# A written-out schedule is replaced by another: two input transfers change places, weights are requested sooner, and the last output halves get a bank each

## The chip, the cores and the metric

The kernel runs on one core of a Trainium2 chip. The metric is the device time of one execution in microseconds (us). Five engines work side by side, each through its own instructions in a fixed order: PE multiplies matrices into PSUM (eight banks), DVE and ACT do elementwise work and empty PSUM, POOL does elementwise work in SBUF and issues some transfers, SP issues the other transfers.

## What is computed

The reference is a gated linear attention over four batches and eight heads of width 48, and a feed-forward layer with SiLU behind it:

```python
f = 1.0 / (1.0 + np.exp(-f_logit))
state = np.zeros((B, H, D, D))
for t in range(S):
    state = f[:, :, t, :, None] * state + np.einsum('bhd,bhe->bhde', k[:, :, t], v[:, :, t])
    y[:, :, t] = np.einsum('bhd,bhde->bhe', q[:, :, t], state)
x = y.transpose(0, 2, 1, 3).reshape(3072, 384)
h = x @ w_in                       # 384 x 2048
out = (h * sigmoid(h)) @ w_out     # 2048 x 384
```

B is 4, H is 8, S is 768, D is 48. The output is 3072 x 384 in float32.

## The kernel before

The sequence is cut into chunks of 128 tokens. A *unit* is one chunk of one batch with all heads, and there are 24; two units make a *pair*, and there are twelve. Pairs 0 to 3 are the first two chunks of one batch each (form T, interleaved tokens), pairs 4 to 11 are the same chunk of two batches (form N).

All work is written out in one table, `PLAN`. A word such as `qg.0.1:G` names the work (`qg`), the pair (0), the unit in the pair (1), the engine (G is POOL, V is DVE, A is ACT, P is PE, S is SP) and, if it makes a new value, the buffer that it takes. The kernel emits the words one after another, so the table fixes the order on each engine. The framework adds the waits between engines. Nothing is reordered later: an instruction that waits holds back all behind it on its engine. The four input transfers that stand first in the table are emitted ahead of the constants.

The words, in the order of the data flow through a pair:

- `f`, `k`, `q`, `v` load the inputs (L241, on SP). `wi` and `wo` load a quarter of `w_in` and of `w_out`, cast to bf16 on the way (L216 and L219, on POOL).
- `E` and `L` (L248, L260, L263) make the logarithm of the gate, `cs` (L324, L331) its running sum on PE, `a` and `ia` (L336) the exponentials of the sum with either sign, `al` (L278, L338) those of the chunk's whole sum.
- `qg` and `ki` (both L341) are the products q by `a` and k by `ia`, on DVE or POOL. `vb` casts v to bf16.
- `tq` (L348) transposes both products on PE, and `qkc` (L185 on ACT, L187 on DVE) copies them out of PSUM; for most later units `qkD` (L360) does both with one transposing transfer.
- `sc` (L369, L373) are the scores, `at` (L377) the masked scores on DVE, `d` (L297, L406) the chunk's addition to the state, `sd` and `su` (L410, L420) the new state, `yi` and `y` (L285, L385, L389) the outputs of the attention, `yc` their cast.
- `yT` and `xc` (L397, L185, L187), or one transposing transfer `yD` (L401), bring them into the layout of the feed-forward layer.
- `mi` (L271) is an eighth of the first layer's product for a pair, into one bank; in pairs 0 and 1 it goes unit by unit. `si` (L276) is its SiLU on ACT. ACT has to load another function table (L513) when it turns from exponentials to SiLU or back.
- `mo` (L306) is a quarter of the second layer's sum for a unit, so four words fill one output bank. `oc` copies it out and `so` (L316, L318) stores it. The last pair's `mo`, `oc` and `so` work on halves of the columns: the fourth number of `mo.11.0.3.1` and the third of `oc.11.0.1` are the half.
- `idle.512.11` runs eleven matmuls without a use (L465).

Buffers rotate: eight PSUM banks `pb`, five exponentials `x`, five products `qk`, and so on. Both halves of the last units' outputs share one bank:

```python
nc.tensor.matmul(at("o", P, i)[:, cols], at("hT", P)[:, n, i * C:(i + 1) * C], w_out_sb[:, n, cols], start=(n == 0), stop=(n == NT - 1))
```

Of the kernel before, what the change touches and what calls it, by code (L numbers as in the profile page):

```python
# [41 lines left out]
tq.1.0:P:2 q.3.0:S:3 a.2.0:A:3 qg.1.1:G: sc.0.0:P:3,4 qkc.1.0:A:1 sc.0.1:P:6,7 at.0.0.1:V:0 k.3.0:S:3 wi.1:G: at.0.0.0:V: E.3.0:A:1 idle.512.2::5
tq.1.1:P:5 at.0.1.0:V:1 wi.2:G: d.1:P:1,4 qkc.1.1:A: v.2.0:S:2 su.1.0:V:0 wi.0:G: at.0.1.1:V: al.2:A:2 L.3.0:A:0 idle.512.3::2 sc.1.0:P:2,3 ki.2.0:G:4
sc.1.1:P:6,1 at.1.0.1:V:2 vb.0.0:A:2 cs.3.1:P:5 vb.0.1:A:3 at.1.1.0:V:3 qg.2.0:G: al.3:A:3 ia.2.1:A:2 d.0:P:7,3 at.1.1.1:V: a.2.1:A:0 cs.3.0:P:6
ia.3.1:A:4 su.0.0:V:0 qg.2.1:G:2 y.0:P:0,1 a.3.0:A:1 at.1.0.0:V: yc.0.0:A:0 yi.0.1:P: tq.2.0:P:7 a.3.1:A:3 wi.3:G: yc.0.1:V:1 ia.3.0:A:0 y.1:P:0,2
wo.0:G: ki.2.1:V: yc.1.0:A:2 yT.0.0:P:5 sd.0.1:V:0 yi.1.1:P: yT.0.1:P:1 yc.1.1:A:0 tq.2.1:P:6 xc.0.0:V:0 wo.1:G: xc.0.1:A: qkc.2.0:V:0 v.3.0:S:3
yT.1.0:P:0 yT.1.1:P:3 xc.1.0:A:1 mi.0.2.0:P:2 qkc.2.1:V: su.0.1:G:0 xc.1.1:A: mi.0.3.0:P:5 mi.1.3.0:P:1 sd.1.1:V:1 mi.1.3.1:P: qg.3.0:V:3 wo.2:G:
mi.0.2.1:P: sc.2.1:P:7,0 si.1.3:A:0 wo.3:G: qg.3.1:V:0 sc.2.0:P:3,6 at.2.1.1:V:0 mi.1.5.1:P:4 mi.1.2.1:P:1 at.2.0.0:V:1 mi.1.2.0:P: at.2.0.1:V:
mi.0.3.1:P: mi.1.4.1:P:0 at.2.1.0:V: mi.1.4.0:P: mi.0.5.0:P:3 si.1.4:A: mi.1.0.0:P:6 mi.1.1.1:P:7 mi.1.0.1:P: f.5.0:S:0 mi.1.5.0:P: si.1.0:A:
mi.0.1.1:P:0 si.0.3:A:1 mi.0.1.0:P: mi.0.5.1:P: si.1.5:A: ki.3.0:G: mi.0.0.0:P:6 si.0.1:A: mi.0.6.0:P:5 mi.0.0.1:P: su.1.1:G:0 mi.0.7.1:P:4 si.0.0:A:  # L50
mi.0.7.0:P: si.0.2:A: mi.0.6.1:P: ki.3.1:G: mi.1.1.0:P: si.0.6:A: mi.1.7.0:P:0 tq.3.0:P:6 mi.1.7.1:P: qkc.3.0:A:1 mi.0.4.0:P:2 tq.3.1:P:5 si.1.7:A:
mi.0.4.1:P: f.4.0:S:1 mo.0.0.0:P:6 qkc.3.1:A: mo.0.1.0:P:0 si.1.1:A: mi.1.6.1:P:5 si.0.5:A: mi.1.6.0:P: si.1.2:A: mo.1.1.0:P:7 si.1.6:A: mo.0.1.1:P:
si.0.4:A: si.0.7:A: sc.3.1:P:3,1 sc.3.0:P:5,2 at.3.1.0:V:2 vb.2.0:A:4 mo.0.1.2:P: at.3.1.1:V: mo.1.1.1:P: at.3.0.0:V:3 mo.0.0.1:P: q.4.0:S:4
mo.0.1.3:P: vb.3.0:V:5 mo.1.1.2:P: vb.3.1:V:6 oc.0.1:V:0 mo.1.1.3:P: at.3.0.1:V: v.5.0:S:4 mo.0.0.2:P: vb.2.1:V:2 v.5.1:S: oc.1.1:V:1 d.2:P:4,3
so.1.1:G: y.2:P:1,5 su.2.0:V:0 v.4.0:S:5 d.3:P:0,2 E.4.0:A:0 sd.2.1:V:0 y.3:P:7,4 yc.3.0:V:1 yi.2.1:P: mo.1.0.0:P:3 L.4.0:A:1 yc.2.1:V:2 yT.3.0:P:7
su.3.0:V:0 mo.1.0.1:P: yc.2.0:V:0 v.8.1:S:0 mo.0.0.3:P: sd.3.1:V:1 yT.2.1:P:5 oc.0.0:A:2 cs.4.0:P:0 k.4.0:S:4 xc.2.1:V:2 yi.3.1:P: a.4.0:A:2 so.0.0:G:
mo.1.0.2:P: ia.4.0:A:1 q.4.1:S: xc.3.0:A:3 yT.2.0:P:1 mo.1.0.3:P: xc.2.0:V: E.5.0:A:1 k.6.1:S:5 mi.2.2:P:2 al.4.0:A:4 cs.4.1:P:6 mi.2.3:P:5 al.4.1:A:5
a.4.1:A:3 q.5.0:S:5 L.5.0:A:2 mi.2.7:P:7 k.5.1:S:0 yc.3.1:A:1 mi.2.4:P:1 ia.4.1:A:0 ki.4.0:G:1 q.5.1:S: mi.2.5:P:0 oc.1.0:A:3 vb.4.0:G:3 yT.3.1:P:4
mi.2.0:P:6 xc.3.1:V: su.2.1:G:0 mi.3.6:P:3 si.2.3:A:2 mi.3.1:P:4 qg.4.0:V: si.2.7:A: k.4.1:S: su.3.1:G:0 si.2.5:A: mi.3.7:P:5 si.3.1:A:3 f.6.0:S:2
mi.2.6:P:7 vb.5.1:A:0 si.3.7:A: d.4.0:P:0 v.4.1:S: mi.2.1:P:4 sd.4.0:V:0 si.2.6:A: qg.4.1:V:2 tq.4.0:P:5 si.2.4:A: mi.3.2:P:0 si.2.1:A: k.7.0:S:1  # L60
si.2.0:A: mi.3.0:P:7 ki.4.1:G: qkc.4.0:A:0 cs.5.1:P:1 mi.3.5:P:4 qkD.4.1:S:1 si.3.0:A: mo.2.1.0:P:6 si.2.2:A: si.3.5:A: sc.4.0:P:5,7 v.7.0:S:1
at.4.0.1:V:0 mo.2.1.1:P: k.5.0:S: at.4.0.0:V: mi.3.4:P:2 q.6.0:S:0 cs.5.0:P:4 ia.5.1:A:4 mo.2.1.2:P: al.5.1:A:1 al.5.0:A:0 ia.5.0:A:1 ki.5.1:V:4
mo.2.0.0:P:7 E.6.0:A:0 vb.4.1:V:1 f.7.0:S:3 mo.2.0.1:P: vb.5.0:A:2 v.9.1:S:3 a.5.1:A:2 mo.2.0.2:P: L.6.0:A:0 qg.5.1:G: d.4.1:P:5 mo.2.0.3:P:
sd.4.1:V:1 a.5.0:A:3 y.4.0:P:1 mi.3.3:P:5 yc.4.0:V:2 su.4.0:G:0 oc.2.0:V:4 mo.2.1.3:P: si.3.3:A: f.8.0:S:1 si.3.4:A: sc.4.1:P:4,1 at.4.1.0:V:1
mo.3.0.0:P:7 si.3.2:A: q.7.0:S:1 oc.2.1:A:5 at.4.1.1:V: cs.6.1:P:5 mo.3.0.1:P: si.3.6:A: y.4.1:P:2 d.5.1:P:0 v.6.0:S:2 yc.4.1:V:0 su.4.1:G:0
mo.3.0.2:P: ia.6.1:A:0 cs.6.0:P:4 k.6.0:S: yT.4.0:P:6 E.7.0:A:1 ki.5.0:V:0 so.2.0:G: mo.3.0.3:P: qg.5.0:V: qkD.5.1:S:2 mo.3.1.0:P:1 L.7.0:A:1
vb.7.0:G:4 mo.3.1.1:P: xc.4.0:A:0 E.8.0:A:0 d.5.0:P:3 yT.4.1:P:2 sd.5.0:V:0 cs.7.0:P:6 mo.3.1.2:P: xc.4.1:A: v.6.1:S: a.6.0:A:4 mi.4.1:P:3 qkD.5.0:S:3
L.8.0:A:2 qg.6.0:G:3 mo.3.1.3:P: ia.6.0:A:2 al.7.0:A:2 mi.4.2:P:2 al.6.0:A:3 oc.3.1:V:1 al.6.1:A:4 a.7.0:A:1 oc.3.0:V:2 ia.7.0:A:3 mi.4.0:P:4 q.6.1:S:
vb.6.0:A:5 ki.6.1:V:1 a.6.1:A:4 sc.5.1:P:1,6 v.7.1:S: at.5.1.0:V:2 mi.4.6:P:7 vb.6.1:G:6 sd.5.1:V:1 mi.4.5:P:5 ki.7.0:G:2 at.5.1.1:V: si.4.6:A:1
mi.4.4:P:1 qg.7.0:G: si.4.0:A: q.8.1:S:2 mi.4.7:P:0 si.4.1:A: y.5.1:P:6 si.4.4:A: mi.4.3:P:7 yc.5.1:V:1 su.5.1:G:0 k.7.1:S: si.4.7:A: cs.7.1:P:4  # L70
si.4.3:A: sc.5.0:P:3,1 k.8.0:S:2 ki.6.0:V: si.4.2:A: mo.4.1.0:P:6 at.5.0.0:V:3 si.4.5:A: q.7.1:S: yT.5.1:P:0 mo.4.0.0:P:7 at.5.0.1:V: mo.4.1.1:P:
qg.6.1:V: al.7.1:A:5 y.5.0:P:2 qkD.6.1:S:0 a.7.1:A:0 cs.8.1:P:5 yc.5.0:A:2 tq.6.0:P:3 ia.7.1:A:3 d.6.0:P:1 qkc.6.0:V:1 vb.7.1:A:3 cs.8.0:P:2
yD.5.0:S:1 mo.4.0.1:P: ia.8.0:A:1 ki.7.1:V:4 ia.8.1:A:2 sc.6.0:P:4,3 qg.7.1:V: al.8.0:A:1 a.8.0:A:4 mo.4.0.2:P: qkD.7.0:S:2 a.8.1:A:3 at.6.0.1:V:0
# [473 lines left out]
```

## Time and profile before

| | |
|---|---|
| time, median of 3 runs | 181.69 us (181.61 to 183.81) |
| the profiled execution's own time | 180.93 us |
| its span | 179.2 us |
| PE busy | 170.5 us (95%) |
| ACT busy | 132.7 us (74%) |
| DVE busy | 79.7 us (44%) |
| POOL busy | 61.6 us (34%) |
| read from HBM, written | 25.17 MB, 4.72 MB |

Times in the rows of the profile count from the start of the span. A row of the timeline has the start, the duration, the engine, the line, the operation with its output and inputs, and in brackets how long the engine had sat idle and what ended that. Matmuls overlap each other, so their durations cannot be added up; the distances between their starts can.

### The profile page before, as it was taken

The numbers are of one execution on the slowest core, as the hardware profiler recorded it, in microseconds if no ns is written. First come the engines' busy times: TensorE is split into PE (matmuls) and PEld (weight loads), VectorE is DVE, ScalarE is ACT, GpSimd is POOL, SyncE is SP. The second block draws the span as 40 slices with busy tenths as digits, with TensorE's granted clock in tenths as the row PEclk, the third lists the DMA queues.
The fourth block names the chain that finished last, engine by engine and source line by source line (L and its number), as shares of the span: only waits on it lengthen the run. The fifth ranks groups of instructions, "written<-read, shape, count | busy, mean of one in ns | idle before, by whom it ended". The sixth has DMA issues, their size and how long they took to land.

```text
span 179.2 us, 4981 instructions
## 1 busy us (share of the span) xinstructions
PE 170.5 (95%) x2042; PEld 129.0 (72%) x2044; DVE 79.7 (44%) x166; ACT 132.7 (74%) x251; POOL 61.6 (34%) x106
## 2 busy tenths in 40 slices
PE   6769989999999999999999999999999999999993
PEld 2345779975788866778678877875876786788782
DVE  7078994008821246456673703342335747500002
ACT  3989983895289999999967558988796991178410
POOL 6036995000274004554044170636303592000010
PEclk9999999999999999999999999999999999999999
DMA  6999999999999799998478998994994496320043
GB/s 159 324 325 325 240 204 207 199 187 190 242 230 212 92 208 221 168 241 144 84 145 170 188 210 141 252 263 103 179 251 94 97 190 215 88 70 0 0 150 117
DMA packets 109366, 31.91 MB, mean 178 GB/s; under 512 B 103536, under 2 KB 108768, under 8 KB 109344
## 3 DMA queue, kind: packets, MB, share of 16 engines
q1 hardware_dynamic: 104464, 25.60, 70.2%
q0 software_dynamic: 4880, 6.00, 15.7%
...
HBM read 25.17 MB, written 4.72 MB: 167 GB/s over the span
## 4 chain that ended last, share of the span: by engine, by line
PE 77%; ACT 9%; DVE 4%; DMA 3%; SPq 2%; issue 1%; POOL 1%; DVEq 0%
PE pb L306 32%; PE pb L271 32%; ACT hT L276 4%; DMA q<-in_q_dram 3%; PE pb L373 2%; SPq L241 2%; PE pb L385 2%; PE pb L348 2%; PE pb L389 2%; DVE qk L341 2%; ACT L513 1%; DVE atm L377 1%; PE pb L331 1%; PE pb L397 1%; DVE st L420 1%
## 5 line engine op out<-in xcount | busy, mean ns | idle before, releaser
L306 PE MATMUL pb<-w_out_sb,hT 128*128 128x384 bf16 (+1 forms) x416 | 70.4, 314 | 0.2 <-ACT hT L276 0.2
L271 PE MATMUL pb<-xT,w_in_sb 128*128 128x256 bf16 (+1 forms) x672 | 68.9, 257 | 0.0
L271 PEld LDWEIGHTS <-w_in_sb 128*128 128x128 bf16 x672 | 56.6, 98 | 7.5 <-issue 0.3
L276 ACT ACTIVATE hT<-pb 128x512 bf16<-128x512 f32 x96 | 51.8, 617 | 12.4 <-PE pb L271 12.0
L306 PEld LDWEIGHTS <-hT 128*128 128x128 bf16 x416 | 37.7, 98 | 18.7 <-ACT hT L276 0.4
L377 DVE TENSOR_TENSOR atm<-pb,triu 128x512 bf16<-128x512 f32 x32 | 20.6, 684 | 20.5 <-PE pb L373 17.8
L336 ACT ACTIVATE x<-pb 128x384 f32<-128x384 f32 x48 | 22.1, 508 | 1.5 <-PE pb L331 1.4
L420 POOL TENSOR_TENSOR st<-sd,al 48x192 bf16<-48x192 f32 x32 | 16.6, 518 | 18.7 <-PE pb L385 12.1
L341 POOL TENSOR_TENSOR qk<-q,x 128x384 bf16<-128x384 f32 x11 | 11.3, 1025 | 31.9 <-ACT x L336 14.5
L513 ACT ACT_TABLE_LOAD x15 | 19.2, 1283 | 0.3
L185 ACT COPY ob<-pb 128x384 f32<-128x384 f32 (+1 forms) x15 | 6.8, 453 | 12.6 <-PE pb L306 12.6
L377 DVE TENSOR_TENSOR atm<-pb,mask 128x512 bf16<-128x512 f32 x16 | 10.2, 685 | 12.4 <-ACT hT L276 11.1
L187 DVE COPY ob<-pb 128x384 f32<-128x384 f32 (+1 forms) x11 | 5.8, 535 | 22.2 <-PE pb L306 22.2
L318 POOL DMA_DIRECT2D out_dram<-ob x8 | 4.6, 578 | 28.4 <-ACT ob L185 24.8
L316 POOL DMA_DIRECT2D out_dram<-ob x14 | 7.6, 548 | 19.6 <-DVE ob L187 15.9
L341 DVE TENSOR_TENSOR qk<-q,x 128x384 bf16<-128x384 f32 x13 | 7.6, 593 | 13.7 <-ACT x L336 13.7
L248 ACT ACTIVATE e<-f 128x768 f32<-128x768 f32 (+1 forms) x13 | 10.4, 800 | 4.4 <-DMA f<-in_f_logit_dram 4.2
L410 DVE TENSOR_TENSOR sd<-pb,st 128x384 f32<-128x384 f32 x16 | 8.9, 554 | 10.6 <-PE pb L406 3.9
L341 POOL TENSOR_TENSOR qk<-k,x 128x384 bf16<-128x384 f32 x10 | 10.8, 1082 | 6.4 <-ACT al L278 2.0
L185 ACT CAST yb<-pb 128x384 bf16<-128x384 f32 x12 | 5.6, 479 | 9.7 <-PE pb L389 9.6
L341 DVE TENSOR_TENSOR qk<-k,x 128x384 bf16<-128x384 f32 x14 | 9.9, 710 | 0.9 <-ACT x L336 0.9
L187 DVE CAST yb<-pb 128x384 bf16<-128x384 f32 x12 | 6.6, 556 | 8.0 <-PE pb L389 5.9
...
## 6 DMA issues: line engine op xcount, KB each, us to landing
...
```

The lines of the kernel that those rows point to most:

```text
L185: nc.scalar.copy(dst, src)
L187: ENG[eng].tensor_copy(dst, src)
L248: return nc.scalar.activation(e, at("f", P)[:, j * w:(j + 1) * w], AF.Exp, scale=-1.0)
L271: nc.tensor.matmul(h[:, i, cols], w_in_sb[:, kk, n * 128:(n + 1) * 128], at("xT", P)[:, kk, cols], start=(kk == 0), stop=(kk == KT - 1))
L276: return nc.scalar.activation(at("hT", P)[:, 2 * j:2 * j + 2, :], at("h", P, j).rearrange("p (n c) -> p n c", n=2), AF.Silu)
L306: nc.tensor.matmul(at("o", P, i)[:, cols], at("hT", P)[:, n, i * C:(i + 1) * C], w_out_sb[:, n, cols], start=(n == 0), stop=(n == NT - 1))
L336: nc.scalar.activation(at(kind, P, i).rearrange("p h d -> p (h d)"), at("cs", P, i)[:, 0:HD], AF.Exp, scale=1.0 if kind == "ia" else -1.0)
L341: ENG[eng].tensor_mul(at("qk", P, i)[:, j, :, 0:D], heads("qk"[j], P, i), at("ia" if j else "a", P, i))
L377: ENG[eng].tensor_mul(at("atm", P, i)[:, r], at(f"s{r}", P, i).rearrange("p (n c) -> p n c", c=C), mask[:, None, :].to_broadcast([C, NP, C]))
L410: nc.vector.tensor_add(at("sd", P, i), d_ps, prev_state(P, i))
L420: ENG[eng].tensor_mul(at("st", P, i)[lo:lo + D, :, r * D:(r + 1) * D], src[lo:lo + D, :, r * D:(r + 1) * D], al_of(P, i)[lo:lo + D, :, Non ...
L513: nc.scalar.preload_act_table_set(TABLES[mode])
```

## The change

The table is replaced by another with the same 879 words, but for the counts of the `idle` words, the engine of 79 others, the buffers and the order. Loads on SP: `q.0.0` is now the second transfer and `k.0.0` the seventh, where it was the other way round, and `f.0.0` comes ahead of `f.0.1`. The first piece of `w_in` (`wi.1`) stands behind two products on POOL. Useless matmuls: 22 instead of 24. POOL gets 27 of the 48 products `qg` and `ki` where it had 21, 8 instead of 5 of the casts `vb` and 18 instead of 15 stores; DVE and ACT give these up. In the last pair each half of an output has its own bank. The core of the diff:

```diff
-f.2.0:S:0 k.0.0:S:0 f.0.1:S:1 f.0.0:S: E.2.0:A:0 f.1.0:S:2 L.2.0:A:0 v.1.0:S:0 q.0.0:S:0 idle.512.11::0 cs.2.1:P:0 E.0.1:A:1 E.0.0:A: k.1.0:S:1
...
+f.2.0:S:0 q.0.0:S:0 f.0.0:S:1 f.0.1:S: f.1.0:S:2 E.2.0:A:0 v.1.0:S:0 L.2.0:A:0 k.0.0:S:0 E.0.0:A:1 idle.512.10::0 cs.2.1:P:0 L.0.0:A:1 k.1.0:S:1
...
-                nc.tensor.matmul(at("o", P, i)[:, cols], at("hT", P)[:, n, i * C:(i + 1) * C], w_out_sb[:, n, cols], start=(n == 0), stop=(n == NT - 1))
+                nc.tensor.matmul(at("o", P, i, *rest[3:])[:, cols], at("hT", P)[:, n, i * C:(i + 1) * C], w_out_sb[:, n, cols], start=(n == 0), stop=(n == NT - 1))
...
-            copy(eng, at("ob", P, i)[:, cols], at("o", P, i)[:, cols])
+            copy(eng, at("ob", P, i)[:, cols], at("o", P, i, *rest[2:])[:, cols])
...
-            return [("o", *rest[:2])]
+            return [("o", *rest[:2], *rest[3:])]
```

On SP the first loads stand as follows (k_65 and q_71 are the buffers of `k.0.0` and `q.0.0`, f_62 is the gate of pair 0, in two transfers; - is before, + the change):

```order
 L241 DMA f_61<-in_f_logit_dram 128x8x96
-L241 DMA k_65<-in_k_dram 128x8x96
+L241 DMA q_71<-in_q_dram 128x8x96
 L241 DMA f_62<-in_f_logit_dram 128x4x96 x2
 L241 DMA f_63<-in_f_logit_dram 128x8x96
 L241 DMA v_77<-in_v_dram 128x8x96
-L241 DMA q_71<-in_q_dram 128x8x96
+L241 DMA k_65<-in_k_dram 128x8x96
 L241 DMA k_66<-in_k_dram 128x8x96
```

The load of q of pair 0 and that of k of pair 0 have changed places; all between them stay.

On POOL, behind the making of the constants, stand the first products and the first weights (q_71 and k_66 are q of pair 0 and k of pair 1, the rows with qk are `qg` and `ki`, w_in_sb is a `wi`):

```order
 masks.py:199 AFFINE_SELECT ident<-ident 128x128
-L187 CAST vb_98<-v_77 128x384
-L341 TENSOR_TENSOR qk_95<-k_66,x_91 128x8x48
-L341 TENSOR_TENSOR qk_96<-q_72,x_92 128x8x48
+L341 TENSOR_TENSOR qk_93<-q_71,x_88 128x8x48
+L341 TENSOR_TENSOR qk_94<-q_71,x_91 128x8x48
+L216 DMA w_in_sb<-in_moe_w_in_dram 128x3x512
+L341 TENSOR_TENSOR qk_96<-q_72,x_89 128x8x48
+L341 TENSOR_TENSOR qk_96<-k_66,x_88 128x8x48
+L187 CAST vb_100<-v_78 128x384
 L216 DMA w_in_sb<-in_moe_w_in_dram 128x3x512 x3
```

`qg.0.0` and `qg.0.1` have come over from DVE to the head of POOL, `qg.1.1` and `ki.1.1` follow, and one piece of `w_in` stands between them; before, three pieces came at once behind two products.

At the end of the program POOL's last instructions before were these (ob is an output buffer, `st` a state; L542 is the end of the program):

```order
L420 TENSOR_TENSOR st_149<-sd_126,al_128 48x4x48 x2
L316 DMA out_dram<-ob_139 64x384 x2
L318 DMA out_dram<-ob_138 128x384
L318 DMA out_dram<-ob_138 128x192
L542 UNCONDITIONAL_BRANCH
```

With the change they are:

```order
L318 DMA out_dram<-ob_139 128x384
L318 DMA out_dram<-ob_134 128x384
L318 DMA out_dram<-ob_135 128x384
L318 DMA out_dram<-ob_139 128x192
L542 UNCONDITIONAL_BRANCH
```

The last store on POOL was `so.11.0.0`, the first half of one unit, whose last word on PE has twelve more behind it; now it is `so.11.1.0`, and its copy `oc.11.1.0` waits for `mo.11.1.3.0`, the last word but one on PE. Of the last pair's other halves, SP stored three before and stores three now, `so.11.0.1` at the very end in both.

More of the change, by code (lines that the diff above doesn't have):

```diff
@@ L42 @@
[L42 to L73, printed above, removed]
@@ new lines @@
+tq.1.1:P:7 at.0.0.1:V:1 vb.0.0:A:3 wi.0:G: tq.1.0:P:6 qkc.1.1:A:1 at.0.0.0:V: d.1:P:1,2 wi.2:G: al.2:A:2 su.1.0:V:0 d.0:P:4,5 qkc.1.0:A: wi.3:G:
+y.0:P:7,0 su.0.0:V:0 yc.0.0:A:0 sd.0.1:V:0 yi.0.1:P: v.2.0:S:2 yc.0.1:A:1 sc.1.0:P:1,6 ia.2.0:A:2 at.1.0.0:V:2 yT.0.0:P:4 sc.1.1:P:7,5 L.3.0:A:1
+ki.2.0:G:4 at.1.1.0:V:3 yT.0.1:P:0 v.3.0:S:3 at.1.0.1:V: cs.3.1:P:3 qg.2.0:G: cs.3.0:P:1 at.1.1.1:V: al.3:A:3 a.3.0:A:0 sd.1.1:V:1 ki.2.1:G:2
+xc.0.1:A:0 idle.512.1::7 tq.2.0:P:7 xc.0.0:V: ia.3.0:A:2 y.1:P:6,5 ia.3.1:A:4 qg.2.1:G: yc.1.0:A:2 mi.0.2.0:P:2 mi.0.3.0:P:0 ki.3.0:V:3 wo.0:G:
@@ new lines @@
+yi.1.1:P: yT.1.0:P:4 tq.2.1:P:1 xc.1.0:A:1 su.0.1:G:0 yc.1.1:A:0 mi.0.3.1:P: qkc.2.1:V:0 mi.1.2.0:P:6 a.3.1:A:1 yT.1.1:P:4 f.4.0:S:0 mi.0.2.1:P:
+xc.1.1:V: ki.3.1:G:0 mi.1.1.0:P:5 mi.0.0.0:P:1 mi.1.1.1:P: wo.1:G: si.0.3:A:0 mi.0.1.0:P:3 qkc.2.0:A: mi.1.2.1:P: qg.3.1:G: mi.0.0.1:P: mi.0.1.1:P:
+si.0.2:A: mi.1.0.0:P:4 wo.2:G: qg.3.0:V: mi.1.0.1:P: si.1.2:A:1 sc.2.0:P:0,7 si.0.1:A: wo.3:G: at.2.0.0:V:0 mi.1.5.1:P:2 si.0.0:A: mi.1.5.0:P:
+at.2.0.1:V: mi.1.4.1:P:6 si.1.0:A: mi.0.4.0:P:3 si.1.1:A: mi.0.4.1:P: mi.0.5.1:P:0 mi.0.7.0:P:1 q.6.1:S:4 mi.1.7.0:P:4 mi.0.6.1:P:7 mi.0.6.0:P:
@@ new lines @@
+qkD.6.1:S:0 tq.6.0:P:2 si.4.3:A: ki.7.0:V:1 mo.4.0.0:P:5 si.4.2:A: vb.6.0:V:6 at.5.0.0:V: d.5.0:P:0 cs.7.1:P:6 mo.4.1.0:P:1 sd.5.0:V:0 at.5.1.0:V:
+cs.8.1:P:4 a.7.1:A:0 y.5.0:P:0 ia.7.1:A:2 qg.7.0:V: mo.4.1.1:P: al.8.1:A:4 a.8.1:A:4 yc.5.0:V:1 ki.7.1:G:0 y.5.1:P:3 qkc.6.0:V:1 yD.5.0:S:1
+mo.4.1.2:P: yc.5.1:A:0 vb.7.1:G:1 a.8.0:A:3 sc.6.0:P:0,2 ia.8.1:A:1 su.5.0:G:0 at.6.0.1:V:0 mo.4.1.3:P: qkD.7.0:S:2 d.6.1:P:3 oc.4.1:A:0 qg.7.1:V:
+yT.5.1:P:4 d.6.0:P:2 ia.8.0:A:2 mo.4.0.1:P: sd.6.0:V:0 su.5.1:G:0 qkD.7.1:S:3 al.8.0:A:0 at.6.0.0:V: sc.6.1:P:1,7 mo.4.0.2:P: so.1.0:G: sd.6.1:V:1
```

90 lines of the change are left out of this document (55 added, 35 removed).

## The prediction

> **What bounds the kernel now.** I read the page first, then PE's waits, then the timeline of the head and the end.
>
> ```profile
> span 179.2 us, 4981 instructions
> PE 170.5 (95%) x2042; PEld 129.0 (72%) x2044; DVE 79.7 (44%) x166; ACT 132.7 (74%) x251; POOL 61.6 (34%) x106
> PE   6769989999999999999999999999999999999993
> ```
>
> PE is busy in all slices from the sixth to the last but one. A busy PE can still hide gaps, so the view of its waits decides (total, times, longest):
>
> ```profile
> PE pb L324 <- ACT lf L260: 1.9, 3, 0.8
> PE pb L465 <- POOL triu masks.py:66: 1.4, 1, 1.4
> PE pb L369 <- issue: 0.9, 1, 0.9
> PE pb L348 <- DVE qk L341: 0.4, 1, 0.4
> PE pb L348 <- POOL qk L341: 0.4, 1, 0.4
> PE pb L306 <- ACT hT L276: 0.2, 1, 0.2
> ```
>
> That is 5.2 us in all. Only the last row, 0.2 us, lies behind the first layers' start; the rest is of the first 27 us. So the kernel is a head, in which the first data make their way to the first `mi`, then some 150 us of PE work without a break, and an end. An order cannot shorten the middle by more than 0.2 us. What it can change is the head, new waits in the middle, and the end.
>
> **The head: the two transfers.** The chain of work at the start runs through the load of q:
>
> ```profile
> 5.24 4.81 DMA q<-in_q_dram
> 10.62 2.31 DVE qk L341 x3
> 13.41 1.01 ACT qkTT L185
> ```
>
> In the change q takes the place of k and lands about 5.3 us, where k did (issue at 1.26 plus 4.0), and k lands at 10.05. But both products need both, and no sooner than the exponentials:
>
> ```profile
> 8.47 0.47 ACT L336 ACTIVATE x<-pb 128x384 f32<-128x384 f32 x1
> 9.57 1.24 ACT L336 ACTIVATE x<-pb 128x384 f32<-128x384 f32 x3
> 10.62 0.55 DVE L341 TENSOR_TENSOR qk<-k,x 128x384 bf16<-128x384 f32 x1
> 11.44 1.06 POOL L341 TENSOR_TENSOR qk<-k,x 128x384 bf16<-128x384 f32 x1 [2.04 <-ACT al L278]
> 11.56 1.36 DVE L341 TENSOR_TENSOR qk<-k,x 128x384 bf16<-128x384 f32 x1
> 13.41 1.01 ACT L185 COPY qkTT<-pb 128x1024 bf16<-128x1024 bf16 x1 [0.48 <-PE pb L348]
> ```
>
> `qg.0.0` can now start at 8.95, when `a.0.0` is done, but `ki.0.1` waits for k until 10.05: the same wait under another name. What helps is that two engines share the four products. `qg.0.1` on POOL waits for `a.0.1` (fourth behind 9.57, 0.41 apart: done at 10.95) and ends at 12.0; DVE's two end at about 11.4; before, the fourth ended at 12.92. ACT then reaches `qkc.0.0` at 13.0 after its own list, not 13.41, as the 0.48 us that it waited for PE goes. The scores begin at 14.2 instead of 14.59: a gain of 0.4 us, no more, since ACT is late next.
>
> A collision stands in these rows: the DVE product took 1.36 instead of 0.55 us while a POOL product ran until 12.50. The Trainium skill, "SBUF — State Buffer", section "Who interferes with whom", says that a DVE instruction with two SBUF inputs and a POOL instruction that reads SBUF exclude each other for the whole instruction; this row agrees, and by the rule each of the four DVE products up to 14 us could lose up to 1 us to POOL's four.
>
> By the 0.8 us of that row I charge `ki.1.0` and `qg.1.0`, which are not the last on their chain. If it hit the two of pair 0, the head would lose what it gained and 0.4 more.
>
> **The head: to the first `mi`.**
>
> ```profile
> 15.06 1.89 DVE L377 TENSOR_TENSOR atm<-pb,mask 128x512 bf16<-128x512 f32 x3 [0.61 <-PE pb L369]
> 19.38 1.64 ACT L336 ACTIVATE x<-pb 128x384 f32<-128x384 f32 x4
> 20.30 0.67 PE L285 MATMUL pb<-vb,atm 64*128 64x48 bf16 x32
> 23.58 1.84 PE L271 MATMUL pb<-xT,w_in_sb 128*128 128x128 bf16 x30
> ```
>
> Before, PE did the scores of both pairs, then `d.0`, then both `y`. Now pair 0 goes ahead: its four `at` (0.6 each from 14.7) end at 17.2, and `y.0` starts at 17.4 instead of 20.3. Pair 1 pays for it. Its second `qkc` on ACT is done at 18.4, its scores stand behind `yi.0.1` (18.7), its four `at` end at 21.8, and `tq.2.0` waits for two POOL products of 1.0 us behind `ia.2.0` (19.9) until 22.0. `y.1` runs from 22.4, the first `mi` from 23.0: 0.6 sooner than 23.58. Of PE's small work, `yi.1.1`, `yT.1.0`, `yT.1.1` and `tq.2.1` are then still to do, about 1.0 us that before was done, with perhaps 0.3 of waiting for `yc.1.0`; in return the 0.85 us at L369 behind 25 us goes. Sum: 0.6 - 1.0 - 0.3 + 0.85, a gain of about 0.2 us. Two useless matmuls less are no gain of their own: they only fill waits. Bounds: a gain of 0.9 (they are 0.43 us each at the start, and as much wait goes with them) to a loss of 1.0 (collisions).
>
> **The weights.** `wi.1` is issued at about 12.0 instead of 15.83 and lands before 20 us.
>
> ```profile
> L216 POOL DMA_DIRECT2D w_in_sb<-in_moe_w_in_dram x1: 937/937/937, 15.8 to 15.8; - x1
> DMA to landing us min/median/max: 7.4/7.4/7.4
> 44.31 0.84 ACT L248 ACTIVATE e<-f 128x768 f32<-128x768 f32 x1 [2.21 <-DMA f<-in_f_logit_dram]
> ```
>
> Before, it landed at 23.2, just ahead of the first `mi`; this wait is covered now by the chain above. The other pieces of `w_in` go at 15.8 to 18 as before. `wo.0` goes two us later, behind four POOL products, at 24.4; in the same queue the pieces landed 2.7 to 3 us apart, so I expect it at about 31, before `mo.0.0.0` at 34.9. All inputs and weights up to the gate of pair 4 move the same bytes as before, so `f.4.0` lands between 42.8 and 44.3. I take nothing for it.
>
> **The middle.** ACT and PE carry the same kinds of work; POOL takes six products of 1.0 us more, beside PE. I take nothing: 150 us of PE work, waits as before. Bounds: a gain of 0.2, a loss of 2.6 (the rival below).
>
> **The end.**
>
> ```profile
> 163.73 0.33 PE pb L306 x4
> 166.67 9.52 PE pb L306 x88
> 171.61 0.32 ACT L185 COPY ob<-pb 128x192 f32<-128x192 f32 x1 [3.65 <-PE pb L306]
> 172.22 0.55 POOL L318 DMA_DIRECT2D out_dram<-ob  x1 [23.40 <-ACT ob L185]
> 176.21 0.32 ACT L185 COPY ob<-pb 128x192 f32<-128x192 f32 x1 [3.29 <-PE pb L306]
> L316 POOL DMA_DIRECT2D out_dram<-ob x2: 537/552/566, 96.3 to 96.9; - x2
> DMA to landing us min/median/max: 2.4/2.5/2.6
> out_dram<-ob POOLq DMA_DIRECT2D x1, 96.0 KB, 2.9
> out_dram<-ob SPq DMA_DIRECT2D x2, 96.0 KB, 1.6
> L542 POOLq DRAIN x3: 46/102/4199, 172.2 to 178.9; - x3
> L542 SPq DRAIN x3: 7/7/13, 178.3 to 178.6; - x3
> ```
>
> The last 88 matmuls ran without a wait in one bank for each unit, so two banks bring nothing here. PE ended at 176.19, the last copy at 176.53, SP's store landed 1.6 later, SP drained at 178.3, and the span ended 0.85 later at 179.2. Now the last copy but one, `oc.11.1.0`, ends at 176.20 (its matmuls are 0.33 ahead), and POOL stores it. POOL issued its last store 0.29 after the copy (171.93 to 172.22), so at 176.5; it lands after 2.5 to 2.9, at 179.0 to 179.4, behind SP's. And POOL's own drain began with that store and took 4.2 us, until 176.4, 1.3 behind the landing. Before, this lay beside PE; now nothing covers it: the drain ends at 180.3 to 180.7, the span 0.85 later at 181.1 to 181.5. I take 181.1, a loss of 1.9, since no other transfer is under way then. Lower bound: only the landing counts, 179.0 against 178.2, a loss of 0.8.
>
> The Trainium skill, "DMA: Bandwidth & Descriptors", section "Latency and other measured facts", gives about 1 us to the first byte from POOL's queue and 0.6 from SP's. By that the end would lose some 0.4 us, and the sum would be +0.2; the rows, 1.6 and 2.5, lie further apart, and none shows the first byte alone.
>
> **The sum**: -0.2 + 0 + 0 + 1.9 = +1.7 us, so 182.6 for the profiled execution with its 180.93. The median of the runs is 0.76 above that execution, which I leave on: 183.4.
>
> **The rivals.**
> - *Only the landing counts* (0.24): the drain that I saw may have stood for something else, as no other is in the trace. +0.8 - 0.2: 182.3.
> - *Not slower* (0.12): the head gains its 0.9, the drain counts for nothing, and the store lands at 178.9, after the shortest 2.4 of the rows, 0.7 behind SP's: -0.9 + 0.7, 181.5. It decides at the first `mi`: before 22.4 us. For it speaks that the planned waits shrank, against it the long list on ACT.
> - *The gate of pair 4 is late* (0.08): `E.4.0` waited 2.2 us before and nothing was behind it; now `vb.3.1` is, which `y.3` needs at about 45.0. If `f.4.0` lands at 44.3 again, `vb.3.1` is done at 45.65: 0.65 more, 184.1. It decides from a landing at 43.6.
> - *A transposing transfer is late* (0.12), which ends slower by over 2%:
>
> ```profile
> L401 SPq DMA_TRANSPOSE xT<-yb x12: 1184/1218/1929, 87.8 to 156.1; - x12
> DMA to landing us min/median/max: 2.3/2.7/5.6
> ```
>
> `yD.6.1` has 3.6 us of PE work between the end of `y.6.1` and `mi.6.5`, less 0.65 for the cast: 2.95. At the median 2.7 it holds; at 5.6, behind loads in SP's order, PE waits 2.65: 186.0.
>
> My forecast has 0.44. That the change does not do what it says is true of the two banks and, for time, of the transfers: it is in the sum.
>
> **Range and chances.** Down from the not-slower case by the 0.2 of the middle and some of the 0.76 between the runs and the profiled execution: 181.0. Up to the forecast with its head and drain at the worst, +1.0 and +2.3 or 185.0, and to some of the late transposition: 185.4. Two per cent, about what a measurement of this kernel tells from no change, are 178.1 and 185.3. Faster by that 0.02, within it 0.85, slower 0.13.
>
> **What would show it.** Right: first scores near 14.2 and first `mi` near 23.0; PE's waits behind 27 us below 0.5; POOL's drain beginning near 176 and lasting some 4 us, with SP done two us before the end. Wrong: a PE wait of over 0.5 in the middle at L271, L285 or L306; a first `mi` outside 22.3 to 24; an end of less than 4 us behind PE's last matmul.

## The result, and the profile after

The changed kernel took **186.99 us** in the median of four runs (185.47 to 188.55), the kernel before 181.94 us beside it: a ratio of **1.0256, interval 1.0209 to 1.0304**, slower by 2.6%. The prediction was 183.4 us, in a range of 181.0 to 185.4. Ratios here compare executions within 1.5% of the fastest of their kernel; where a median lies far above its ratio, longer executions are in the median alone.

The profiled execution took 185.47 us, 4.54 more than that of before, and was the shortest of the four. The head of its page, as the page of before was shown:

```profile
span 183.6 us, 4986 instructions
PE 170.8 (93%) x2042; PEld 128.6 (70%) x2042; DVE 75.8 (41%) x158; ACT 132.9 (72%) x250; POOL 70.2 (38%) x118
PE   7577799999999999998997999999999999999990
```

PE is as busy as before in us, but two slices in the middle are no longer full (the 8 near 85 us and the 7 near 100 us), and the last is empty. Five of the nine rows of PE's waits (total, times, longest):

```profile
PE pb L324 <- ACT lf L260: 2.9, 4, 1.0
PE pb L271 <- DMA xT<-yb: 1.1, 1, 1.1
PE pb L297 <- DVE atm L377: 0.7, 2, 0.4
PE pb L385 <- DVE st L420: 0.5, 1, 0.5
PE pb L373 <- ACT hT L276: 0.3, 1, 0.3
```

The rows at L271 and L373 are new and lie behind the head, where only 0.2 us at L397 joins them. The one at L373 shows only a part of its stall; the timeline has the rest (start, duration, engine, operation):

```profile
79.99 0.48 ACT L185 COPY ob<-pb 128x384 f32<-128x384 f32 x1 [1.03 <-DMA out_dram<-ob]
80.48 1.28 ACT L513 ACT_TABLE_LOAD   x1
81.78 3.04 ACT L276 ACTIVATE hT<-pb 128x512 bf16<-128x512 f32 x6
82.74 0.88 PE L373 MATMUL pb<-qkT 48*128 48x128 bf16 x9
83.89 0.38 PE L373 MATMUL pb<-qkT 48*128 48x128 bf16 x7 [0.28 <-ACT hT L276]
84.38 0.81 PE L271 MATMUL pb<-xT,w_in_sb 128*128 128x256 bf16 x6
97.47 0.62 PE L373 MATMUL pb<-qkT 48*128 48x128 bf16 x16
98.02 1.48 PE L271 MATMUL pb<-xT,w_in_sb 128*128 128x256 bf16 x12
100.56 2.14 PE L271 MATMUL pb<-xT,w_in_sb 128*128 128x256 bf16 x18 [1.06 <-DMA xT<-yb]
```

*Stall A.* ACT's copy `oc.3.1` waits 1.03 us for output buffer 5, whose store `so.2.0` is still under way. The table load and six SiLU come later by that, and the scores of pair 5 (`sc.5.0`, `sc.5.1`) wait for the banks that these empty: their 16 matmuls take from 82.74 to 84.38, 1.64 us, where the next 16 take 0.55 (97.47 to 98.02). That is a loss of 1.1 us. *Stall B.* `mi.6.5` waits 1.06 us for the transposing transfer `yD.6.1`.

The end of the program; `x2` is the two last copies, both on ACT:

```profile
172.00 7.06 PE L306 MATMUL pb<-w_out_sb,hT 128*128 128x384 bf16 x72
178.77 0.65 ACT L185 COPY ob<-pb 128x192 f32<-128x192 f32 x2 [1.33 <-PE pb L306]
179.38 0.54 POOL L318 DMA_DIRECT2D out_dram<-ob  x1 [5.90 <-ACT ob L185]
```

The drains at the program's last line (ns, then the first and last start):

```profile
L542 POOLq DRAIN x3: 46/93/3480, 179.4 to 183.3; - x3
L542 SPq DRAIN x3: 7/7/7, 181.6 to 183.1; - x3
```

PE ends at 179.06, 2.9 us later than before. The last two stores, issued at 179.38 on POOL and 179.44 on SP, land 2.06 and 1.65 us later, at 181.44 and 181.09, and POOL's drain of 3.48 us, which begins with that store, ends at 182.84, 1.4 behind the landing. The span ends 4.5 us behind PE, before it was 3.0. So the 4.4 us of span are 2.9 on PE's path (1.1 + 1.1 for A and B, 0.3 at the first `mi`, at 23.90 instead of 23.58, 0.3 ahead of `mi.11.0`, 0.1 elsewhere) and 1.5 behind it.

### The profile page after: what moved, and what is told of

Its sections match the earlier page's. It is cut to its first block, busy times and chain, and to the rows that moved or that the text cites. A ratio compares the mean times of both kernels' runs of the same rounds, so it can differ in the third digit from the quotient of the medians.

```text
span 183.6 us, 4986 instructions
## 1 busy us (share of the span) xinstructions
PE 170.8 (93%) x2042; PEld 128.6 (70%) x2042; DVE 75.8 (41%) x158; ACT 132.9 (72%) x250; POOL 70.2 (38%) x118
## 4 chain that ended last, share of the span: by engine, by line
PE 56%; ACT 11%; DMA 11%; issue 7%; DVE 7%; POOL 5%; SPq 2%; POOLq 0%; ACTq 0%; DVEq 0%
PE pb L271 23%; PE pb L306 22%; DMA xT<-yb 4%; DVE atm L377 3%; ACT hT L276 3%; POOL qk L341 3%; DMA out_dram<-ob 3%; DMA f<-in_f_logit_dram 2%; ACT x L336 2%; DMA v<-in_v_dram 2%; PE pb L385 2%; ACT e L248 2%; PE pb L348 2%; SPq L241 2%; PE pb L389 2%
## 5 line engine op out<-in xcount | busy, mean ns | idle before, releaser
L271 PE MATMUL pb<-xT,w_in_sb 128*128 128x256 bf16 (+1 forms) x672 | 68.9, 257 | 1.3 <-DMA xT<-yb 1.1
L276 ACT ACTIVATE hT<-pb 128x512 bf16<-128x512 f32 x96 | 51.2, 604 | 19.8 <-PE pb L271 19.2
L271 PEld LDWEIGHTS <-w_in_sb 128*128 128x128 bf16 x672 | 57.2, 98 | 9.8 <-DMA xT<-yb 1.8
L341 POOL TENSOR_TENSOR qk<-k,x 128x384 bf16<-128x384 f32 x14 | 14.0, 998 | 29.3 <-issue 10.6
L341 POOL TENSOR_TENSOR qk<-q,x 128x384 bf16<-128x384 f32 x13 | 13.6, 1046 | 25.6 <-DMA q<-in_q_dram 12.7
L318 POOL DMA_DIRECT2D out_dram<-ob x11 | 6.2, 563 | 25.4 <-ACT ob L185 25.4
L316 POOL DMA_DIRECT2D out_dram<-ob x14 | 7.7, 554 | 13.2 <-ACT ob L185 13.2
L185 ACT CAST yb<-pb 128x384 bf16<-128x384 f32 x15 | 7.3, 489 | 6.6 <-PE pb L389 5.4
L341 DVE TENSOR_TENSOR qk<-q,x 128x384 bf16<-128x384 f32 x11 | 8.3, 764 | 5.6 <-DMA q<-in_q_dram 3.6
L465 PE MATMUL pb<-zero,triu 128*128 128x512 bf16 x22 | 7.2, 461 | 1.4 <-POOL triu masks.py:66 1.4
L341 DVE TENSOR_TENSOR qk<-k,x 128x384 bf16<-128x384 f32 x10 | 6.2, 649 | 5.2 <-ACT x L336 3.6
```

The costliest lines, as they stand in the source:

```text
L185: nc.scalar.copy(dst, src)
L271: nc.tensor.matmul(h[:, i, cols], w_in_sb[:, kk, n * 128:(n + 1) * 128], at("xT", P)[:, kk, cols], start=(kk == 0), stop=(kk == KT - 1))
L276: return nc.scalar.activation(at("hT", P)[:, 2 * j:2 * j + 2, :], at("h", P, j).rearrange("p (n c) -> p n c", n=2), AF.Silu)
L316: ENG[eng].dma_start(out=dst.rearrange("(p j) n -> j p n", j=2)[j], in_=ob[j * HC:(j + 1) * HC])
L341: ENG[eng].tensor_mul(at("qk", P, i)[:, j, :, 0:D], heads("qk"[j], P, i), at("ia" if j else "a", P, i))
```

## Experiments

All runs are timed against the kernel before, in the same comparison (medians of before 181.4 to 181.6 us, and 181.94 beside the change). "Above" is the difference of the medians.

| run | median, us | lowest to highest | above, us | ratio, interval |
|---|---|---|---|---|
| the change | 186.99 | 185.47 to 188.55 | 5.1 | 1.0256 (1.0209 to 1.0304) |
| end on SP | 184.06 | 182.84 to 186.50 | 2.5 | 1.0118 (1.0066 to 1.0169) |
| another output buffer | 185.49 | 183.33 to 188.38 | 3.9 | 1.0110 (1.0054 to 1.0166) |
| transposition ahead of loads | 186.30 | 185.22 to 188.37 | 4.7 | 1.0230 (1.0180 to 1.0279) |
| these three together | 183.75 | 182.65 to 184.47 | 2.2 | 1.0101 (1.0057 to 1.0145) |
| and `wi.1` back | 182.97 | 182.65 to 183.49 | 1.5 | 1.0079 (1.0059 to 1.0099) |
| before, last store on POOL | 183.31 | 183.12 to 183.54 | 1.8 | 1.0096 (1.0079 to 1.0113) |
| before, swap and banks | 181.56 | 180.90 to 182.31 | 0.0 | 0.9989 (0.9966 to 1.0012) |
| before, `wi.1` sooner | 182.15 | 181.64 to 188.82 | 0.6 | 1.0021 (1.0005 to 1.0037) |
| all mended | **181.15** | 181.01 to 182.11 | -0.4 | **0.9984** (0.9971 to 0.9997) |
| the change, `wi.1` back alone | 183.94 | 183.84 to 184.86 | 2.4 | 1.0134 (1.0111 to 1.0157) |
| the change, more distance | 184.08 | 183.32 to 186.42 | 2.6 | 1.0115 (1.0089 to 1.0142) |
| the change, products later | 184.98 | 184.44 to 186.79 | 3.6 | 1.0229 (1.0186 to 1.0272) |
| all mended, `wi.1` sooner | 183.68 | 182.33 to 184.67 | 2.2 | 1.0120 (1.0074 to 1.0166) |
| that, products later | 181.65 | 181.50 to 183.57 | 0.2 | 1.0027 (0.9999 to 1.0054) |

**The end on SP.**

```diff
-so.11.1.0:G:
+so.11.1.0:S:
```

> The changed kernel, but its last store but one, so.11.1.0, is issued by SP and not by POOL. In the changed kernel the span ends 4.5 us behind PE's last matmul, before the change 3.0 us. Theory (POOL's drain sets the end): the end shrinks to about 3.0 us, the kernel gains 1.5 us and stands 3.0 to 3.6 us above the kernel before (ratio 1.017 to 1.020). Rival (only the landing counts, 181.44 on POOL against 181.09 on SP): a gain of 0.35 us, ratio 1.023 to 1.026.

The drain of POOL in this run:

```profile
L542 POOLq DRAIN x3: 46/93/3753, 172.7 to 181.9; - x3
```

It begins at 172.7 again, beside PE, and the span of 182.2 us ends 3.3 us behind PE (178.9) instead of 4.5: 1.2 us gained, near the theory's 1.5, far from 0.35. The 0.3 left against before does not come from the two last copies, though they stand behind each other on ACT: the last ends 0.35 us behind PE in both kernels. SP now issues the two last stores behind each other, the last one 0.12 instead of 0.03 us behind its copy, and SP's drain begins 0.26 instead of 0.14 us behind the landing. The median fell by more, 2.6 us against the change; four runs of the change don't settle such a difference.

**The last store of the kernel before on POOL.** The same term in the other kernel:

```diff
-so.11.0.1:S:
+so.11.0.1:G:
```

> The kernel before, but its very last store, so.11.0.1, is issued by POOL and not by SP. Theory (POOL's drain ends some 3.5 us behind its last issue): the span ends 1.9 to 2.6 us later, ratio 1.010 to 1.014. Rival (only the later landing counts, 0.3 later issue and 0.4 longer): 0.7 to 0.9 us, ratio 1.004 to 1.005.

The same row of this run:

```profile
L542 POOLq DRAIN x3: 46/93/3238, 177.4 to 181.1; - x3
```

The store, issued at 177.4, lands 1.9 us later at 179.3; the drain ends at 180.6, and the span of 181.4 us 4.7 us behind PE (176.7) instead of 3.0. By the medians the edit costs 1.8 us; the interval of 1.0079 to 1.0113 leaves out the 0.7 to 0.9 us of the landing alone. So the drain is a cost of its own, a little smaller than expected.

**Another output buffer.** `so.1.1` is moved behind `so.0.0`, and buffers 0 and 5 change places from `oc.3.1` on:

```diff
-oc.3.1:A:5
+oc.3.1:A:0
...
-oc.4.1:A:0
+oc.4.1:A:5
```

> The changed kernel, but so.1.1 stands right behind so.0.0 on POOL and oc.3.1 takes output buffer 0, which so.1.1 has emptied long before, and not buffer 5, whose store so.2.0 is still under way (the two buffers change places in all later words). Theory: ACT's 1.03 us of waiting for that store at 79 us goes, the table load and the six SiLU behind it come 1.0 us sooner, PE's stall of 1.15 us at the scores of pair 5 (82.7 to 84.4 us) goes: a gain of 1.0 to 1.15 us. Rival 1: ACT is late there anyway, by its own list: a gain under 0.3. Rival 2: PE comes sooner, but the transposing transfer yD.6.1 lands when it did, and the wait at mi.6.5 grows from 1.1 to 2.1 us: no gain.

ACT's wait for the store is gone and so is every wait at L373. But this execution, one of the longer ones with 187.73 us, lost time elsewhere, in the head (from its timeline):

```profile
23.33 0.34 DVE L187 COPY xT<-pb 128x384 bf16<-128x384 bf16 x1
28.20 0.56 DVE L341 TENSOR_TENSOR qk<-k,x 128x384 bf16<-128x384 f32 x1 [4.53 <-DMA k<-in_k_dram]
28.67 0.68 DVE L187 COPY qkTT<-pb 128x1024 bf16<-128x1024 bf16 x1
29.41 2.84 PE L271 MATMUL pb<-xT,w_in_sb 128*128 128x128 bf16 x48 [1.77 <-DVE qkTT L187]
```

DVE stood 4.53 us at `ki.3.0`, for the load `k.3.0`; the copy `qkc.2.1` behind it empties a bank, and PE waited 1.77 us for that bank. In the changed kernel's own trace DVE waits 1.5 us at this place and PE not at all. The times don't tell the theory (1.0 to 1.15) from the first rival; the trace confirms the cause of stall A and shows a second loss.

**The transposition ahead of two loads.**

```diff
-k.10.0:S:3
...
-q.9.0:S:3
...
 yD.6.1:S:
+k.10.0:S:3
+q.9.0:S:3
```

> The changed kernel, but the loads k.10.0 and q.9.0 stand behind the transposing transfer yD.6.1 on SP and not ahead of it. Theory: these two loads, issued 2.9 to 3.5 us ahead of the transfer and landing at 97.1 and 97.7 us, made it land 4.0 us behind its issue where the median of the twelve is 2.5; without them it lands in 2.5 us, PE's wait of 1.1 us at mi.6.5 is gone, a gain of 1.1 us. Rival: the transfer is late because its cast on ACT is (behind a table load of 1.28 us) or for the stores under way; then it still takes over 3.5 us and the gain is under 0.3 us.

The theory falls: the transfer, issued at 98.79, still took 3.8 us, PE still waited 0.82 us, and the median hardly moved. In the traces of the change and of eleven variants of it, with the loads ahead or behind, `yD.6.1` took 3.1 to 4.1 us. This trace shows something else behind stall A, which is longer in it (ACT waits 1.78 us for the store; each stretch: us, busy time of PE, PEld, DVE, ACT and POOL, granted clock, DMA share, GB/s):

```profile
82.00:84.00 2.00, 1.34 (x15) 0.82 (x14) 0.00 (x0) 1.99 (x5) 0.46 (x1) 1.00 0.99 202
84.00:86.00 2.00, 1.53 (x19) 1.25 (x19) 1.63 (x3) 1.59 (x5) 0.00 (x0) 0.99 1.17 268
86.00:88.00 2.00, 2.00 (x15) 1.32 (x13) 1.09 (x3) 1.98 (x3) 0.00 (x0) 0.50 1.24 244
88.00:90.00 2.00, 2.00 (x22) 1.19 (x21) 1.62 (x3) 1.18 (x3) 0.40 (x1) 0.65 0.04 9
```

After four us in which PE was busy 1.34 and 1.53 of 2.00, the granted clock was 0.50 and then 0.65, so in this execution of 188.37 us stall A was followed by a loss of up to 1.7 us more, (1 - 0.50) x 2 + (1 - 0.65) x 2. In the profiled execution of the change the clock stayed at 1.00 in these stretches, with PE busy 1.61 and 1.89.

**The three together.** The edits above in one kernel.

> The changed kernel with the three edits together: last store but one on SP, another output buffer for oc.3.1, the transposing transfer ahead of two loads. Theory (three separate losses on PE's path, of 1.5, 1.1 and 1.1 us): a gain of 3.7 us, so 0.6 to 1.4 us above the kernel before (ratio 1.003 to 1.008). Rival (one loss hides another, and some of it is given back at a later wait): a gain of 2.5 us or less, ratio above 1.011.

Neither: 2.2 us above, between 1.4 and 2.5. The waits for the store and for `yD.6.1` are gone from the trace. DVE still waited 2.0 us for `k.3.0` and 2.5 for `q.3.0`.

**And `wi.1` back to its place.**

```diff
-wi.1:G:
...
+wi.1:G:
 wi.0:G:
```

> The kernel with the three edits together, and wi.1 back to its place before the change (with the other pieces of w_in, behind four POOL products). Theory (the piece that is issued sooner takes bandwidth from k.3.0 and q.3.0, so that DVE, which has ki.3.0 ahead of a copy that PE's banks wait for, waits 1.5 to 4.5 us for the load at 25 us): k.3.0 lands by 23.5 us instead of 25 to 28, DVE's wait falls below 0.5 us, and the median falls by 0.3 to 1.0 us, since only some executions had a wait of PE behind it. Rival (the loads are late for another reason): k.3.0 lands when it did, the median moves by less than 0.3.

DVE's waits for the loads are gone, the median falls by 0.8 us, and highest and lowest run are 0.8 us apart instead of 1.8. As the theory has it. What remains shows in the timeline:

```profile
105.46 0.84 ACT L248 ACTIVATE e<-f 128x768 f32<-128x768 f32 x1 [1.22 <-DMA f<-in_f_logit_dram]
109.14 2.12 PE L271 MATMUL pb<-xT,w_in_sb 128*128 128x256 bf16 x18 [0.90 <-ACT hT L276]
162.57 1.48 PE L271 MATMUL pb<-xT,w_in_sb 128*128 128x256 bf16 x12 [0.86 <-DMA xT<-yb]
```

The first two rows are a price of my own edit: two loads moved behind `yD.6.1` made `f.9.0` late, and ACT waits for it ahead of the SiLU; only the three traces with the moved loads have this wait of ACT. The third is `mi.11.0`, which waits for `yD.11.1`: stall C, of 0.3 us in the changed kernel.

**Swap and two banks alone,** in the kernel before:

```diff
-f.2.0:S:0 k.0.0:S:0 f.0.1:S:1
+f.2.0:S:0 q.0.0:S:0 f.0.1:S:1
...
-mo.11.1.0.1:P:
+mo.11.1.0.1:P:3
```

> The kernel before with the two named edits alone: the loads k.0.0 and q.0.0 change places, and the second halves of the last pair's outputs get a bank of their own (3 and 4); no other word moves. Theory (as in the prediction: the first wait changes its name, and the last matmuls never waited for a bank): within 0.3 us of the kernel before, ratio 0.998 to 1.002. Rival: ki.0.1 on DVE, which stands behind qg.0.0, waits for k until 10.05 us and all of DVE's list behind it with it, or the first products come sooner: 0.4 us or more in one of the two directions.

Nothing, as the theory had it: two of the three edits that the change is named after have no effect on the time by themselves.

**`wi.1` sooner alone,** in the kernel before:

```diff
 vb.1.1:G:0
+wi.1:G:
...
-wi.1:G:
```

> The kernel before, but wi.1 stands right behind the cast vb.1.1 on POOL, ahead of two products, and is issued at 10 to 12 us instead of 15.8. Theory: k.3.0 and the loads behind it land 1 to 4 us later than the 21.1 us of before, but in this order no instruction ahead of PE's work waits for them: within 0.4 us, ratio 0.998 to 1.002. Rival (the loads of pair 2 and 3 are late for PE too): 1 us or more above, ratio 1.005 or more.

Seven of twelve executions took 181.64 to 182.18 us, near what the theory had; their ratio of 1.0021 lies just above its range. The other five took 185.54 to 188.82, where none of the 23 executions of the kernel before was over 183.55. The profiled execution was of the first kind: `k.3.0` landed at 27.64 us instead of 21.11, and no wait of PE came of it. What the five longer ones waited for is not shown.

**All mended.** The end on SP with its copy on DVE, the buffers exchanged, `wi.1` back, and more of PE's work between two transpositions and their first use, for which three words of `mi.11` change banks; the loads stay where the change has them. A part of the diff:

```diff
-oc.11.1.0:A:
+oc.11.1.0:V:
...
-mi.6.5:P:6 si.5.5:A: at.7.0.1:V: v.8.0:S: mi.5.6:P:4 si.6.5:A:3
+si.5.5:A: at.7.0.1:V: v.8.0:S: mi.5.6:P:4
...
 mi.5.4:P:2
+mi.6.5:P:6
...
-mi.11.0:P:0
+mi.10.5:P:0
+mi.11.0:P:4
```

> The changed kernel with five edits: so.11.1.0 stored by SP, its copy oc.11.1.0 on DVE beside the last one on ACT, the output buffers exchanged as before, wi.1 back to its old place, and more work of PE between the last two transposing transfers and their first use (mi.6.5 goes behind mi.5.6 and mi.5.4, which are 1.3 us; mi.10.5 goes ahead of mi.11.0, 0.65 us); the loads k.10.0 and q.9.0 stand where the change put them. Theory (the distance in the plan was too short, not the loads ahead of the transfer): PE waits for no xT, PE's waits behind 27 us are under 0.5 us, the end is 0.3 us shorter, and the time is 180.7 to 182.0 us, ratio 0.995 to 1.003. Rival (what remains above the kernel before, 0.8% with the three first edits and the weights, is spread over the new order and not in these waits): ratio above 1.005.

181.15 us, 0.36 below the kernel before; the interval ends at 0.9997. All of PE's waits:

```profile
PE pb L324 <- ACT lf L260: 2.0, 3, 1.0
PE pb L465 <- POOL triu masks.py:66: 1.4, 1, 1.4
PE pb L369 <- ACT qkTT L185: 0.9, 1, 0.9
PE pb L385 <- DVE st L420: 0.5, 1, 0.5
PE pb L297 <- DVE atm L377: 0.2, 1, 0.2
PE pb L397 <- DVE yb L187: 0.2, 1, 0.2
```

No wait for `xT` or `hT` is left, and behind 27 us only the 0.2 at L397. The theory holds for the waits and the time, and this version is as fast as the kernel before, or a little faster: the difference is far under 2%. The end did not become shorter: the span still ends 3.4 us behind PE (179.6 against 176.2), so the copy on DVE brought nothing.

**Two parts alone, in the changed kernel.** First `wi.1` in its old place:

> The changed kernel, but wi.1 stands in its old place on POOL, behind four products and with the other pieces of w_in. Theory (the piece issued sooner makes k.3.0 and the loads behind it late, and some executions wait for them on PE): the median falls by 0.5 to 1.2 us and highest and lowest run come closer than the 3.1 us of the changed kernel, ratio 1.018 to 1.023. Rival (the gain seen with the three other edits came from elsewhere): the median moves by less than 0.3 us.

Then the distances of `mi.6.5` and `mi.10.5`:

> The changed kernel, but mi.6.5 goes behind mi.5.6 and mi.5.4, and mi.10.5 ahead of mi.11.0; all else stands. Theory (a transposing transfer takes 3.1 to 4.0 us at these two places, and the changed plan leaves 2.95 and 3.2 us of PE's work for it): PE's waits for xT are gone, a gain of 1.1 to 1.5 us, ratio 1.017 to 1.020. Rival (the later first words of pair 6 and 11 hold back SiLU and the second layer behind them): a gain under 0.5 us.

Each brought some 2.5 us in the median, more than either theory; the change has four executions, so the 2.5 us are rough. In the second run PE's waits for `xT` are gone from the trace. In the first they stand in the timeline at both places, longer than in the change:

```profile
99.60 2.14 PE L271 MATMUL pb<-xT,w_in_sb 128*128 128x256 bf16 x18 [1.15 <-DMA xT<-yb]
162.62 1.48 PE L271 MATMUL pb<-xT,w_in_sb 128*128 128x256 bf16 x12 [0.55 <-DMA xT<-yb]
```

The highest of five executions with `wi.1` back took 184.86 us; of six with more distance, two took 186.4.

**Products later.** Is it DVE's order? `wi.1` is issued as soon as the change has it:

```diff
-ki.3.0:V:3
...
 xc.1.1:V:
+ki.3.0:V:3
...
-qg.3.0:V:
...
 at.2.0.1:V:
+qg.3.0:V:
```

> The changed kernel with wi.1 issued as soon as the change has it, but on DVE the product ki.3.0 stands behind the copies qkc.2.1 and xc.1.1, and qg.3.0 behind at.2.0.0 and at.2.0.1; both are wanted only by the transposition tq.3.0 some ten us later. Theory (the loads k.3.0 and q.3.0, late because of wi.1, hold back on DVE what PE's banks wait for): PE has no wait at 27 to 32 us in any execution, the median falls to 183.5 to 185.0 us, nearly what wi.1's old place gave (183.94), ratio 1.011 to 1.019. Rival (wi.1 harms in another way, by the loads of pair 2 or by the pieces of w_out on POOL behind ki.3.1 and qg.3.1): the median stays above 186 us, ratio above 1.022.

The median is at the theory's upper end, the ratio above it. Two of the six executions took 186.6 and 186.8 us. This does not decide, with stalls A, B and C in it.

**The same question with all else mended.** Only `wi.1` differs from the kernel with all five edits:

> The kernel with all five edits, of 181.15 us, but wi.1 is issued at 12.3 us as the change has it; nothing else differs. Theory (wi.1 ahead of its time is a loss of its own, by way of the late loads of pair 3): a median of 182.0 us or more, some executions of 184 us or more, ratio above 1.003. Rival (it did harm only together with the other waits, whose margins it used up): 180.9 to 181.6 us, ratio 0.996 to 1.001.

And with the two products later on DVE:

> The same, with wi.1 issued at 12.3 us, and ki.3.0 and qg.3.0 on DVE behind the copies and masked scores that PE waits for. Theory (the harm of wi.1 goes by way of DVE, which waits for k.3.0 and q.3.0 in its order): 180.9 to 181.6 us with highest and lowest run within 1.2 us of each other, ratio 0.996 to 1.001. Rival (it goes another way, by POOL's products and the pieces of w_out behind them, or by the loads of pair 2): as the run without this edit, some executions of 184 us or more.

This decides the first question: 183.68 against 181.15 us, so `wi.1` costs **2.5 us** by itself. Of these, the two products give back 2.0 (181.65): most of the harm goes by DVE's order. In the first of the two runs DVE stood twice at a load, in the second never:

```profile
26.41 0.64 DVE L341 TENSOR_TENSOR qk<-k,x 128x384 bf16<-128x384 f32 x1 [2.38 <-DMA k<-in_k_dram]
30.52 0.56 DVE L341 TENSOR_TENSOR qk<-q,x 128x384 bf16<-128x384 f32 x1 [2.61 <-DMA q<-in_q_dram]
```

Three of the twelve executions of the second run still took 182.65 to 183.57 us. They are those with the lowest mean granted clock, 0.981 to 0.990; the other nine have 0.997 or more. In the profiled execution of the first run (182.44 us) PE waited nowhere behind the head but for 0.2 us at L397; what its trace shows as a loss is a dip of the granted clock:

```profile
18.00:20.00 2.00, 1.35 (x63) 1.25 (x66) 1.85 (x6) 0.93 (x3) 0.40 (x1) 1.00 1.16 299
20.00:22.00 2.00, 2.00 (x40) 1.30 (x32) 1.44 (x3) 1.52 (x3) 1.12 (x2) 0.51 1.22 226
22.00:24.00 2.00, 2.00 (x23) 1.12 (x20) 2.00 (x5) 0.87 (x3) 2.00 (x3) 0.64 1.21 206
```

A dip is not the whole loss: the two longest executions of this run, 184.52 and 184.67 us, have a mean granted clock of 0.997. They were not traced, so that PE waits there behind DVE follows from the gain by the two products and is not seen.

## Why the prediction was wrong

**What bounds the kernel** was read rightly: head, PE's work without breaks, end. But from it I drew "I take nothing" for the middle. That before had no waits there bounds only the gain.

**The swap and the banks** were taken at nothing, and are nothing (0.9989).

**The head.** The scores began at 14.17 (forecast 14.2), the first `mi` at 23.90 (forecast 23.0, with 22.3 to 24 as what it could be). The difference is the collision, which I had charged to `qg.1.0` at 0.8 us, as one that does no harm there:

```profile
13.30 1.01 POOL L341 TENSOR_TENSOR qk<-q,x 128x384 bf16<-128x384 f32 x1
13.72 1.97 DVE L341 TENSOR_TENSOR qk<-q,x 128x384 bf16<-128x384 f32 x1
14.26 1.01 POOL L341 TENSOR_TENSOR qk<-k,x 128x384 bf16<-128x384 f32 x1
15.61 2.47 DVE L377 TENSOR_TENSOR atm<-pb,mask 128x512 bf16<-128x512 f32 x4
18.45 0.58 PE L285 MATMUL pb<-vb,atm 64*128 64x48 bf16 x32
```

`qg.1.0` took 1.97 instead of 0.55 us beside two products on POOL. I had it as "not the last on their chain", but the masked scores of pair 0 stand behind it on DVE: they began at 15.61 instead of 14.7, and `y.0` at 18.45 instead of 17.4. The rule of the Trainium skill that the prediction named ("SBUF — State Buffer", "Who interferes with whom") fits this row.

The collision in this size comes with `wi.1`, whose issue stands ahead of the two products on POOL. In all nine traces of the new order with `wi.1` issued at 12.1 to 12.5 us, `qg.1.0` took 1.97 to 1.99 us; in the three with `wi.1` in its old place it took 0.62 to 0.78. With `wi.1` back alone the head came almost as forecast:

```profile
13.64 0.64 DVE L341 TENSOR_TENSOR qk<-q,x 128x384 bf16<-128x384 f32 x1
17.41 0.59 PE L285 MATMUL pb<-vb,atm 64*128 64x48 bf16 x32
23.33 0.84 PE L271 MATMUL pb<-xT,w_in_sb 128*128 128x128 bf16 x12 [0.40 <-DMA w_in_sb<-in_moe_w_in_dram]
```

The last row shows the price of the old place: the first `mi` waits 0.4 us for the piece, and without that wait it would have begun at 22.9.

**The weights: the step that failed most.** I followed `wi.1` and the last load of the stretch, and both came as forecast: `wi.1` was issued at 12.34 us and landed 6.2 later, and the gate of pair 4 landed at 42.88. From equal sums of bytes I concluded "I take nothing for it". The loads between were not looked at. The row of `k.3.0` (issue to landing; issued at 14.01 in the changed kernel, at 13.93 in the one with all mended), first the change, then all mended:

```profile
DMA to landing us min/median/max: 10.9/10.9/10.9
```

```profile
DMA to landing us min/median/max: 6.2/6.2/6.2
```

So `k.3.0` lands at 24.95 instead of 20.1, and `q.3.0` behind it at 30.42 instead of 21.2. The product that waits for `k.3.0` stands on DVE ahead of copies that PE's banks wait for. Measured, with all else equal: 2.5 us (183.68 against 181.15) where the sum had 0. Not each execution pays it: PE did not wait there in the profiled one of the change, and the median lies 1.5 us above it, not the 0.76 that I left on. Which part of this 1.5 is the waits and which a dip of the clock stays open: the three executions without a trace have a mean granted clock of 0.982 to 0.991, the traced one 0.995.

**The middle.** Measured in the profiled execution: 2.5 us (A 1.1, B 1.1, C 0.3) where I took 0, inside my bound of 2.6. B is the fourth rival at the place it named, with 1.06 us where it had 2.65: the slack of 2.95 us was right, the transfer took 4.0. I gave it 0.12 because the median of all twelve transfers, 2.7 us, held. At this place it was never the median: 3.1 to 4.1 us in twelve traces, and 3.5 in that of before, where more work lay in between. A, the reuse of an output buffer whose store is under way, I had not thought of; nothing in the trace of before shows it, but the table does: when `oc.3.1` came, five of the six buffers were full and the sixth in its store, which took 4.4 to 4.6 us.

**The end.** This term held: +1.5 us where I took 1.9, and 1.8 when the last store of the kernel before went to POOL. The rival "only the landing counts" is out. The 0.4 us by the Trainium skill ("DMA: Bandwidth & Descriptors", "Latency and other measured facts") would have been too little: landings of 2.06 and 1.65 us differ by just 0.4, but the drain comes on top.

**The other rivals.** The gate of pair 4 landed at 42.88, under the 43.6 from which it decides, and PE had no wait at `y.3`. "Not slower" fell with the head.

So the sum of +1.7 us had the end right, the head about 0.5 too low (by way of `wi.1`), and two terms at nothing that measured 2.5 us each: the weights in the median, the middle in the profiled execution. In the medians they do not add up: with `wi.1` sooner and all else mended 2.2 of the 5.1 us remain, so the other edits are worth 2.9, of which the end is 1.5 to 1.8 and A, B and C 1.1 to 1.4. That a later PE waits less for the same landing would account for it; no run tests this.
